# Attention and a gated feed-forward block on one core: query and key transposes of the later tiles moved from TensorE to DMAs, in a newly planned order

## The chip, the cores and the metric

One core of a Trainium2 chip. The time is the device's microseconds for one execution, as the median of several runs; "span" is the profiled execution from its first to its last instruction, about 1.8 us shorter than the time. Each kernel was measured in the same rounds, and on the same chip, as the kernel before, and the ratios quoted are to that one (its medians: 271.45 to 271.49). Two other kernels, of different rounds, are compared through it; the last run was on another chip than the rest of the experiments.

## The reference

```python
# q, k, v: (4, 8, 768, 64); heads 0, 2 and 6 see all earlier keys,
# the other five only the first 4 keys and the last 64
scores = q @ k^T / 8, masked; a = softmax(scores)
x = (a @ v) laid out as (3072, 512)
g = x @ w_gate                      # 512 x 1536
silu = g / (1 + exp(-g))
return (silu * (x @ w_val)) @ w_out # 1536 x 512, float32 out
```

The kernel works in fp16 with float32 sums. Attention is cut into 12 pairs of 128-query tiles (24 tiles); four tiles make a group, and the feed-forward products of a group run on TensorE between the attention work of later tiles.

## The kernel before

Every instruction is a named task. A planner, run beforehand, fixed the order of all tasks (`ORDER`) and for each task the engine that does it (`WAYS`); the kernel holds both as encoded strings and issues accordingly, so each engine's instruction stream is fixed. The parts that matter here:

```python
XBAR = 12                      # tiles from 12 on: output transposed by a DMA on SyncE
RINGS = {"raw": 11, "hq": 2, "e": 7, ...}   # buffers in rotation

def cast(n, kd, j):            # q or k of pair n: float32 as loaded -> fp16 in hq
    ...
    copy(T_c[n, kd, j], hqs[n][:, "qk".index(kd), j]..., r[:, :, j]...)

def transposes(n, w):          # w = 0: queries, 1: keys; 8 transposes on TensorE
    for j in range(2):
        for p in range(4):
            nc.tensor.transpose(tr[...], hqs[n][:, w, j, p // 2, ...], ident)

def evac(n):                   # PSUM -> qT, its two half-zero copies (one each)
    copy(T_ev[n, 0], qT[n % 2][0:64, 0]..., trs[n, 0][0:64])
def evac1(n):
    copy(T_ev[n, 1], qT[n % 2][64:128, 1]..., trs[n, 0][64:128])
def evack(n, x, ps):           # PSUM -> kT
    ...
# small copies that gather sink and window blocks (names used below):
#   sk, sv   sinks of k and v       pk, pv   previous blocks of k and v
#   cx       v as loaded -> fp16    ex       exponentials (ScalarE only)
#   mask     product of e with a mask
```

A task's `ways` say which engines could do it: `copy` tasks may go to ScalarE, VectorE or GpSimd, exponentials only to ScalarE.

The softmax here doesn't subtract the row's maximum and nothing guards it: scores larger than these inputs give would overflow.

Of the kernel before, what the change touches and what calls it, by code (L numbers as in the profile page):

```python
# [16 lines left out]
    "000701060803091Ixq040A1J1L1K02050By81T1V1N1O0C1Uy81Q1o1S1R1M0D2cxy1W1p1r1q1w1X0E1z1P1x1e1y2d2021"  # L17
    "0G1Y1g1Z1f1v1a4D1b1h0H1txs1i101c1s1j220F1d1k2Y2X231l0Pxs1m2a1u242A2514130I1n26272Z9c2B9m280N9w11"
    "9n292E9d9o2C9e4E9x0L2F9f2D9p9y9g9z2b0J9q2G4AA0A62H49A94B0M2IA72JA8xo9h1A0KAA9r9i9k9s9j179tA10O9l"
    "AB4CA29uACA3ADA40Q1D1G9vAE160RAFAG1CA5AL480SAH2KAJAM19AI2LAK0T2S2MAQ2T2N1F2UAR0U2RAN2Q2V2P2WAO3M"  # L20
    "2OAS0V2g2e3L38ATAP2h39AV0X3A2jAU3BAa2i2k0a3G3C3F2mAY3I2n3D0WAW3H2o152u2fAX3J0Y3E2pAd2v1EAZ3K0c2x"
    "Ab122yAcAf2l0b18302w2q31Ai0Z2rAg3N3PAe3v322s3QAkAh2z0dAj3w3O3SAl33An3T2tAp1B0e1H43Am3VAq34453R3W"
    "As0f443y3XAu353U3YAo3x360g3Z42373f403a463g3zAvAr0hAt4G3i3b473jAw3c4w0i4F3h3dAx3l4jAz3k3m0j3e3pB0"
    "4k3q4p414r4l0k3n5WB13o4n4s4HB24x3r4m4tB44I5Y0l4u4K4o3s5dB55c4v4L0m4z3tB63u4J4NBE0n4O4yBJ625X5bBH"
    "630oBF4VBKBG4M5e4WBL4P0pBM685a4Y69BOBI674ZB3BN4qBTBP6L64BRBQBU4Q664bBWBV4cAy4a5g4RBYBS4S504XBZBb"
    "BX51BaBd5ZBc5253B75fBgBeB8Bf4TB9655A54BA0q5B5672BBBhBiBn55BjBC0r57Bl6sBo4d58594eCC6v0s6uBk5G4fBp"
    "6t5HBsBm0t6N744gBx4U5C5IBy0u4h5DBqBt4i5JBu5hBD5KBr5QBvBz5MBwC05N0v5iC25L6o5OC1C35ECD6r6p5PC55R5j"
    "5F0w5SC46qC76K5T5kC65UCAC87e5V7fC96ACW7g0xCB8C8OCbCX6CCZCY0y5lCeCcCECd7d0zCaCg8ACf89ClCh8QCjCi8B"
    "5rCFCq955sCHCG6BCr8wCk8x6D8yCm5mCI6E5n5t716w5uCJCn5v6M8vCo5x5wCtCK7Z5yCLCM7aCp975z6xCsCN606G6FCv"
    "Cu7cD06ICwCy6H6JCx6OD1COCz6PD25oD36Q5p6R7bD45qD56SDAD66T6UD8DBD76VDC6W6b6XDD6cD9DF616d6eDGDIDECP"  # L30
    "6jDHCRDK6k6f6y6YDN6Z6h6a6g6z6iCS7085DJ75DLCT8788766l868GCUDPDM6m78CQDQDSDO79776nDU8H7B947kDR7CDV"
    "DT7F737l7DDW7E7A8P7KDX7h7G7LDZCV7j7H7NDY7I8rDo7O8tDa8N7P7iDr7Q8u7M7JDbDp7RDqDtDsDy8sDuDwDc7U8D7V"
    "DeDvDd7SDf8EE3Dz7TDgE08FE8DxE47mE5E1E97WEAED7n7XE6E2EE7o8zEFEIE7EBEJEGEKEC7p7Y7uEN7vEHEL7qEOEQDh"
    "7xEP7w7rDj91ES7sDiEMDkETER7t7y80EUEX907zEc81EYDlEd828J8IEeEV8KEZDm8R83Eh8M8S84EaEW8UEbEiEm8L8VEj"
    "Ef8T8XEk8Y8e928f8ZEnEg938gF6FBElF78h8WFGFCF8EoFD96F9FHFIFEDnFAFLFF8iFJ8aFM8m8j8k8nFQ8lFN8b988cFV"
    "99FK8oFR9BFOFWFS9CFXFT8d9AEpFaFU9DErFbFP9E8pEs9I9FEtFYEu9GFd9HEq9N9J8qEwFc9K9OEx9L9P9QFf9R9XFZEy"
    "9Y9SFkEvEzFe9TFgF0Fp9UFhF19MFqFl9VFi9WF29ZFmF39aFnFr9bFjFsF4FuFtG4FoFvFzG5G0FxFwF5G2G1FyGOG3GTGP"
    "G6GQGUGYGVG7GRGZG8G9GSGdGaGAGeGWGfGbGXGgGcGBGhGiGCGnGlGjGEGkGoGpGsGmGxGtGqGuGyGvGzGrH2GwH7H3H0H8"
    "H4GFH9GDH5HAH6H1GGHBHCHHHDHFHEGHHMHGGIHIHKHJHNHLHOHPHRGJHSGKHTGLHQHUHWHVHXGMHYGNHbHZHcHaHdHeHf"
)  # L40
WAYS = (
    "000000000000000000000000000000000000000000000000000000000000000001002010021000112002001001000100"
    "000000000000000020011000001000000000000000000000100011100000010011101100100100000000001000000000"
    "000100100000000000000000000000000000010000000000000000000110000001000001100100000000000000000000"
    "000000000000001000001000000000000000000000010000000000101011010000000100000000001000001101000000"
    "100101000000000000000000000100000000000100001001000111100000100000000000000000000000000000011011"
    "000000000000000000000010101010100001000101000000100000000000000000000011020100110110100010000000"
    "000000010000000000000000000000000000000000000000000000000000000000000000000000000000000000000000"
    "000000000000100000000010000000000000000000000000000000000000000000000000000000000000000000000000"
    "000000000000000000000000000000000000000000000000000000000000000000000000000000000100000000000000"  # L50
    "000000000000000000000000000000000000000000000000000000000000000000000010000000000000000000000000"
    "000000000000000000000000000000000000000100000000000000100000000000000000000000000000000000000000"
    "0000000000000000000000000000100001000000"
# [55 lines left out]
def kernel(  # L109
# [37 lines left out]
    HALVES = 4  # L147
    NG = len(SIZES)
# [8 lines left out]
    RINGS = {"raw": 11, "hq": 2, "e": 7, "xb": 3, "xt": 2, "sig": 2, "sil": 3, "ahead": 3,  # L157
             "h": 2 * NJ, "osb": 2, "gv": 3, "o": 1, "sc": 1, "av": 1, "tr": 1}
# [100 lines left out]
    def mask_fill():  # L259
        ps = mask_ps.pop()  # L260
        for dst, src in ((m2[:, 0:1], OWN), (m2[:, 1:4], DIAG), (m2[:, 4:5], FAR),
                         (m1[:, 0:2], OWN), (m1[:, 2:4], FAR),
                         (m0[:, 0:2], DIAG), (m0[:, 2:7], BAND0), (m0[:, 7:8], DIAG)):
            nc.vector.tensor_scalar(  # L264
                out=dst, in0=ps[:, src].unsqueeze(1).to_broadcast([128, dst.shape[1], 128]),
                scalar1=-1.0 / OFF, op0=ALU.mult, scalar2=1.0, op1=ALU.add)
# [6 lines left out]
    qT = [const.tile([128, 2, 4, 2, 128], FH, name=f"qT{n}") for n in range(2)]  # L273
    k2 = [const.tile([128, 4, 4, 128], FH, name=f"k2_{n}") for n in range(2)]
# [12 lines left out]
    def fill2():  # L287
        for n in range(2):
            nc.vector.memset(k2[n], 0.0)  # L289
            nc.vector.memset(v2[n], 0.0)  # L290
# [13 lines left out]
    T_fill2 = P.add("fill2", [("DVE", 4.0, 4.0, 0)], -0.5, fill2, after=[T_fill0])  # L304
    T_mord = P.add("mord", [pe(0.216)], -0.5, mask_order, deps=[T_masks], takes=["tr"])
    T_fill = P.add("mfill", [("DVE", 2.4, 2.4, 0)], -0.4, mask_fill, deps=[T_mord])
    P.uses(T_mord, "tr", T_fill)
# [32 lines left out]

    T_load, T_seq = {}, {}
    T_dma = P.add("dma", [("SP", 4.8, 4.8, 0)], -9.0, lambda: None)
    for at, (kd, n) in enumerate(order):
        d = {"q": 1.78, "k": 1.78, "x": 1.78}.get(kd, 1.42)
        T_load[kd, n] = P.add(
            f"load {kd}{n}", [("SP", d, d + (0.9 if at < 5 else 2.0), 0)], at * 1e-2 - 5,
            (lambda kd=kd, n=n: load(kd, n)), after=[T_dma, T_seq.get("load") if kd in "qkx" else None],
            takes=["raw"], grp=f"L{n if kd in 'qkx' else kd}")
        if kd in "qkx":
            T_seq["load"] = T_load[kd, n]  # L350
# [4 lines left out]
    def wcast(kind, n):  # L355
        r = landed.pop((kind, n))
        if kind == "o":
            dst, src = wo_sb[:, 2 * n:2 * n + 2, :], r.rearrange("p (a n) -> p a n", a=2)
        else:
            dst = (wg_sb if kind == "g" else wv_sb)[:, :, n * 256:(n + 1) * 256]  # L360
            src = r.rearrange("p (a n) -> p a n", a=4)
        copy(T_w[kind, n], dst, src)

    for n in range(6):
        for kd in "gvo":
            pos = 0.9 + n / 10 if kd == "o" else n / 6 - 0.3
            T_w[kd, n] = P.add(
                f"wc {kd}{n}", [pool(1.04), act(1024), both(0.75)], pos,
                (lambda kd=kd, n=n: wcast(kd, n)), deps=[T_load[kd, n]])
            P.uses(T_load[kd, n], "raw", T_w[kd, n])  # L370


    A = 0.25

    XBAR = 12

# [9 lines left out]
    def cast(n, kd, j):  # L386
# [3 lines left out]
        r = landed[kd, n].rearrange("p (h j d) -> p h j d", j=2, d=64)  # L390
        copy(T_c[n, kd, j],
# [4 lines left out]
    def castv(n, m, j):  # L396
# [3 lines left out]
             r[m * 64:(m + 1) * 64, :, j])  # L400

# [16 lines left out]
    def evac(n):  # L418
        copy(T_ev[n, 0], qT[n % 2][0:64, 0].rearrange("c p j n -> c j p n"),
             trs[n, 0][0:64])  # L420
# [6 lines left out]

    def evac1(n):
        copy(T_ev[n, 1], qT[n % 2][64:128, 1].rearrange("c p j n -> c j p n"),
             trs[n, 0][64:128])  # L430
# [26 lines left out]
    def plan(t):  # L457
# [3 lines left out]
        if i == 0:  # L461
            at = enumerate(((0, 0), (2, 2), (3, 4), (1, 6)))
            return [([(p, (0, 1), c, 0) for _, (p, c) in at], 8, m0)]
# [16 lines left out]
    def marks(t, u):  # L480

        if t >= LEAD:
            return []
        if TILES[t][1] == 0:
            return [(0, DIAG, 2), (2, BAND0, 2), (4, BAND0, 3), (7, DIAG, 1)]
# [18 lines left out]
    scs, whole_sc, es, av_blocks = {}, {}, {}, {}  # L504

    def scores(t, u, unit):
        if (t, u) == (1, 0):
            sc = [buf("gv", [128, 4, 128], FP, "sc") for _ in range(2)]
# [3 lines left out]
        scs[t, u] = sc  # L512
# [14 lines left out]
    def exps(t, u, unit):  # L527
        sc = scs.pop((t, u))
# [6 lines left out]
        if (t, u) == (1, 0):  # L535
            for x in range(2):
                nc.scalar.activation(
                    out=e[:, 4 * x:4 * x + 4], in_=sc[x], func=AF.Exp, scale=scale)
        else:
# [384 lines left out]
```

## Time and profile before

271.49 us (271.47 to 271.74, 3 runs), span 269.7 us. The table gives the first four stretches of 20 us. "Wanted" TensorE work is the count of matmuls of each shape in the stretch, times (columns / 2400 + 0.0025) us, without the filler matmuls; matmuls shown on the edge of a stretch count in both, so a stretch can read up to 0.4 us too high. The other columns are busy time.

| stretch, us | TensorE wanted | ScalarE | GpSimd |
|---|---|---|---|
| 0 to 20 | 6.27 | 11.18 | 13.23 |
| 20 to 40 | 14.73 | 16.10 | 14.92 |
| 40 to 60 | 18.30 | 19.68 | 14.85 |
| 60 to 80 | 19.18 | 17.70 | 12.99 |
| every later full one | 20.1 to 20.5 | | |

### The profile page before, as it was taken

To read this page: it belongs to the slowest core of one execution; us is meant where nothing else is said; L and a number is where in the kernel's file an instruction comes from. 1 tells how busy PE (TensorE), PEld (TensorE's weight loads), DVE (VectorE), ACT (ScalarE), POOL (GpSimd) and SP (SyncE) were. 2 spreads that over 40 slices of the span, in tenths; PEclk is the share of its full clock that TensorE was granted. 3 is DMA by queue.
4 is the path that set the end of the run, shared out by engine and by line. 5 is a ranking of instruction groups with operands and counts; after the bars stand their busy time and mean duration, and the time that the engine had idled before them with its cause. 6 is when DMAs were issued, how large, how long until landed. Compare 5 with 4: busy or idle time off the path is not lost.

```text
span 269.7 us, 5353 instructions
## 1 busy us (share of the span) xinstructions
PE 257.9 (96%) x2063; PEld 150.2 (56%) x2063; DVE 173.6 (64%) x340; ACT 167.1 (62%) x260; POOL 113.0 (42%) x145
## 2 busy tenths in 40 slices
PE   7799889899999999999999999999999999999993
PEld 7777546465655565455566655555555554444441
DVE  6757787896679487666668257764582565555321
ACT  2499779999897668767757974486564613141300
POOL 6679936774786541876523233366320200000000
PEclk9999999999999999999999999999999999999999
DMA  7999999999950999011114210102014220110144
GB/s 193 295 347 349 332 280 357 341 288 290 289 158 11 256 310 277 8 40 41 39 21 98 61 39 19 41 19 62 1 23 96 59 59 3 39 39 0 41 102 93
DMA packets 55801, 36.52 MB, mean 135 GB/s; under 512 B 8160, under 2 KB 51168, under 8 KB 55776
## 3 DMA queue, kind: packets, MB, share of 16 engines
q1 hardware_dynamic: 55696, 36.05, 50.4%
q8 instruction: 16, 0.26, 0.4%
q10 hardware_dynamic: 80, 0.13, 0.2%
q14 instruction: 9, 0.07, 0.1%
HBM read 28.31 MB, written 6.29 MB: 128 GB/s over the span
## 4 chain that ended last, share of the span: by engine, by line
PE 80%; ACT 12%; DVE 5%; issue 2%; ACTq 0%
PE gv L761 42%; PE o_ps L790 21%; PE sc L524 9%; PE av L557 5%; ACT e L540 4%; PE tr L413 3%; ACT v L178 2%; ACT hq L178 2%; ACT sig L767 1%; ACT vt L178 1%; DVE m L264 1%; PE xtr L582 1%; DVE v L290 1%; DVE k L289 1%; DVE wg_sb L180 1%
## 5 line engine op out<-in xcount | busy, mean ns | idle before, releaser
L540 ACT ACTIVATE e<-sc 128x1024 f16<-128x1024 f32 (+4 forms) x67 | 60.9, 909 | 22.9 <-PE sc L524 22.5
L761 PE MATMUL gv<-xt,wg_sb 128*128 128x512 f16 (+1 forms) x304 | 71.7, 368 | 1.7 <-DVE wg_sb L180 1.2
L761 PE MATMUL gv<-xt,wv_sb 128*128 128x512 f16 (+1 forms) x304 | 72.3, 368 | 0.0
L548 POOL TENSOR_TENSOR e<-e,m 128x640 f16<-128x640 f16 (+1 forms) x25 | 44.5, 1787 | 66.0 <-ACT e L540 65.9
L790 PE MATMUL o_ps<-wo_sb,h 128*128 128x512 f16 x288 | 71.8, 379 | 0.3 <-ACT o_sb L178 0.3
L767 ACT ACTIVATE sig<-gv 128x512 f32<-128x512 f32 (+1 forms) x76 | 43.1, 575 | 44.6 <-PE gv L761 42.6
L771 DVE SCALAR_TENSOR_TENSOR sil<-sig,gv 128x512 f32<-128x512 f32 (+1 forms) x76 | 49.5, 656 | 31.6 <-ACT sig L767 31.1
L778 DVE SCALAR_TENSOR_TENSOR h<-sil,gv 128x512 f16<-128x512 f32 (+1 forms) x76 | 48.8, 655 | 9.6 <-PE gv L761 8.5
L761 PEld LDWEIGHTS <-wg_sb 128*128 128x128 f16 x304 | 28.9, 98 | 29.3 <-DVE wg_sb L180 1.4
L761 PEld LDWEIGHTS <-wv_sb 128*128 128x128 f16 x304 | 28.7, 98 | 26.6 <-issue 0.2
L790 PEld LDWEIGHTS <-h 128*128 128x128 f16 x288 | 26.6, 98 | 26.3 <-issue 0.5
L524 PE MATMUL sc<-qT,kT 128*128 128x256 f16 (+1 forms) x228 | 35.2, 257 | 1.4 <-ACT e L540 0.8
L180 POOL COPY v<-vt 32x528 f16<-32x528 f16 (+1 forms) x46 | 29.4, 639 | 6.5 <-ACT vt L178 3.8
L524 PEld LDWEIGHTS <-kT 128*128 128x128 f16 x228 | 20.6, 98 | 13.3 <-issue 2.7
L180 POOL CAST vt<-raw 64x512 f16<-64x512 f32 x30 | 18.6, 623 | 16.1 <-DMA raw<-in_v_dram 11.2
L557 PEld LDWEIGHTS <-e 128*128 128x128 f16 x472 | 20.1, 97 | 7.5 <-issue 0.5
L565 DVE RECIPROCAL rc<-av 128x4 f32<-128x4 f32 x48 | 8.6, 180 | 24.0 <-PE av L557 23.6
L178 ACT CAST hq<-raw 128x512 f16<-128x512 f32 x32 | 19.3, 617 | 4.3 <-DMA raw<-in_q_dram 3.0
L557 PE MATMUL av<-vt,e 128*128 128x65 f16 x392 | 21.7, 193 | 0.2 <-DVE xb L566 0.2
L566 DVE TENSOR_TENSOR xb<-av,rc 128x256 f16<-128x256 f32 x48 | 20.4, 424 | 1.7
L413 PE MATMUL tr<-ident,hq 128*128 128x128 f16 x192 | 15.0, 219 | 2.1 <-DVE m L264 1.0
L413 PEld LDWEIGHTS <-hq 128*128 128x128 f16 x192 | 12.2, 98 | 5.7 <-DVE m L264 1.2
(57 smaller groups left out, 191.8 us busy)
## 6 DMA issues: line engine op xcount, KB each, us to landing
raw<-in_q_dram SPq DMA_DIRECT2D x12, 512.0 KB, 7.2
raw<-in_k_dram SPq DMA_DIRECT2D x12, 512.0 KB, 7.1
raw<-in_v_dram SPq DMA_DIRECT2D x12, 512.0 KB, 7.4
out_dram<-o_sb SPq DMA_DIRECT2D x47, 128.0 KB, 2.3
raw<-in_moe_w_gate_dram SPq DMA_DIRECT2D x6, 512.0 KB, 8.7
raw<-in_moe_w_val_dram SPq DMA_DIRECT2D x6, 512.0 KB, 8.7
raw<-in_moe_w_out_dram SPq DMA_DIRECT2D x6, 512.0 KB, 7.5
xt<-xb SPq DMA_TRANSPOSE x12, 2.4
```

Of the source, the lines that this page charges most:

```text
L178: nc.scalar.copy(out=dst, in_=src)
L180: ENG[task.way[0]].tensor_copy(out=dst, in_=src)
L413: nc.tensor.transpose(tr[:, p, :, j, :] if w else tr[:, j, p, :], hqs[n][:, w, j, p // 2, (p % 2) * 128:(p % 2 + 1) * 128], ident)
L524: nc.tensor.matmul(sc[c // 4][:, c % 4:c % 4 + n, :], weights, moving, start=first, stop=last)
L540: nc.scalar.activation(out=e[:, 0:n], in_=whole_sc.pop((t, u))[:, 0:n], func=AF.Exp, scale=scale)
L548: ENG[task().way[0]].tensor_tensor(out=ev, in0=ev, in1=mm, op=ALU.mult)
L557: nc.tensor.matmul(av[:, n, 0:65], ee, vv, start=(m == 0), stop=(m == len(bl) - 1))
L761: nc.tensor.matmul(ps, wsb[:, kk, j * 128:(j + 1) * 128], xt[:, kk, c[0]:c[1]], start=(kk == 0), stop=(kk == 3))
L767: nc.scalar.activation(out=sg[g, j, c], in_=gs[g, j, c], func=AF.Tanh, scale=0.5)
L771: nc.vector.scalar_tensor_tensor(out=sl[g, j, c], in0=sg.pop((g, j, c)), scalar=1.0, op0=ALU.add, in1=gs.pop((g, j, c)), op1=ALU.mult)
L778: nc.vector.scalar_tensor_tensor(out=hs[g, j][:, c[0]:c[1]], in0=sl.pop((g, j, c)), scalar=0.5, op0=ALU.mult, in1=vs.pop((g, j, c)), op1=A ...
L790: nc.tensor.matmul(o_open[g, tt], hs[g, j][:, tt * 128:(tt + 1) * 128], wo_sb[:, j, :], start=(j == 0), stop=(j == NJ - 1))
```

## The change

Intent: take the transposes of the late pairs off the full TensorE and give them to DMAs, which issue from SyncE and write straight to SBUF. Queries of pairs 5 to 11 and keys of pairs 8 to 11 go this way (the outputs of the last twelve tiles already did). The plan was made anew, with SyncE's issue and the transfer behind it costed apart, and with smaller units at the start.

```diff
 ORDER, WAYS: all new
-    RINGS = {"raw": 11, "hq": 2, "e": 7, ...}
+    RINGS = {"raw": 11, "hq": 2, "e": 6, ..., "queue": 4}
+    hqz = const.tile([128, 2, 2, 4, 128], FH, name="hqz")   # zero-padded queries
+    XQK = 5
+    XK = 8
 def cast(n, kd, j):
+        if n >= XQK and kd == "q":
+            for s_ in range(2):        # two half-size casts, each into its padded place
+                copy(T_c[n, kd, j], hqz[:, j, s_]..., r[:, :, j]...)
+            return
+    def dmaq(n, j):
+        nc.sync.dma_start_transpose(
+            out=qT[n % 2][:, :, :, j].rearrange("c s p n -> c (s p) n"),
+            in_=hqz[:, j].rearrange("p s a x -> p (s a x)"))
+    def dmak(n, j):
+        ...
+        for m in range(2):
+            nc.sync.dma_start_transpose(out=kT[b % 2][:, :, at:at + 64],
+                in_=hqs[n][m * 64:(m + 1) * 64, 1, j].rearrange("p r x -> p (r x)"))
 # at the start: tiles 0 and 1 scored in half-size units; first gate and value
 # weights cast in halves; memsets of k2, v2 split into four (one on GpSimd);
 # normalisations of tiles 0 to 3, and copies of transposed outputs, may go to
 # ScalarE; pair 2's loads ahead of most weight loads
```

## The prediction

> **What bounds the kernel now.** I read the page first (busy shares, slices), then the stretches of 20 us, then the chain of waits, then TensorE's waits and the transposes' own row. The page says that TensorE is the engine to look at, and that its clock is granted in full throughout:
>
> ```profile
> PE 257.9 (96%) x2063; PEld 150.2 (56%) x2063; DVE 173.6 (64%) x340; ACT 167.1 (62%) x260; POOL 113.0 (42%) x145
> PE   7799889899999999999999999999999999999993
> ACT  2499779999897668767757974486564613141300
> PEclk9999999999999999999999999999999999999999
> DMA  7999999999950999011114210102014220110144
> ```
>
> The reader should see two stages: up to about slice 12 (80 us) TensorE has holes while ScalarE and the DMAs are near full; from there TensorE is full and nothing else is. The stretches say the same in microseconds:
>
> ```profile
> 20.00:40.00 20.00, 17.33 (x168) 12.13 (x166) 15.20 (x37) 16.10 (x28) 14.92 (x22) 1.00 1.09 321
> 40.00:60.00 20.00, 19.06 (x174) 11.46 (x173) 17.42 (x32) 19.68 (x31) 14.85 (x17) 1.00 1.12 328
> 80.00:100.00 20.00, 20.00 (x179) 11.86 (x178) 14.80 (x32) 14.51 (x23) 12.13 (x10) 1.00 0.68 177
> 200.00:220.00 20.00, 20.00 (x153) 10.90 (x152) 10.76 (x23) 9.20 (x14) 3.09 (x2) 1.00 0.26 59
> ```
>
> "Busy" TensorE need not be TensorE at its rate, so I checked the rate. In the timeline, 8 transposes start at 56.17 and the next matmul at 56.62: 0.45 us for eight, 56 ns each, although the table below gives 219 ns as the length of one. In the chain, 56 projections of 512 columns take 12.10 us, 216 ns each. Both fit columns/2400 us plus 2.5 ns. With that spacing and the counts by shape the whole program is: 832 full-width projections 179.6, 64 of 256 columns 7.0, 196 score products of 256 columns 21.4 and 80 of 128 columns 4.5, mask products 2.3, 472 value products 14.0, 192 transposes of queries and keys 10.7, 48 of outputs 2.7, together **242.3 us** of wanted work (156 filler matmuls apart). TensorE's last matmul ends at 265.1 us in the chain of waits. So 22.8 us of TensorE time are lost. Counting the same way by stretch, 13.7 us are lost before 20 us, 5.3 in 20 to 40, 1.7 in 40 to 60, 0.8 in 60 to 80, and nothing measurable after that: each later stretch of 20 us holds 20.1 to 20.3 us of work. TensorE's waits confirm that they are few and early:
>
> ```profile
> PE gv L761 <- DVE wg_sb L180: 1.2, 1, 1.2
> PE tr L413 <- DVE m L264: 1.0, 1, 1.0
> PE sc L524 <- ACT e L540: 0.8, 2, 0.6
> PE tr L413 <- ACT sig L767: 0.7, 1, 0.7
> ```
>
> **What the Trainium skill says.** "VectorE: DVE Perf Modes", The three transpose paths, gives 390 ns for one 128x128 transpose on TensorE and 1309 ns by DMA, so one by one the DMA looks worse. The trace agrees that a single DMA transpose is slow (2.4 us from issue to landing, but for four blocks), yet in this pipeline a TensorE transpose holds TensorE for 56 ns, not 390; that is what counts here. "TensorE: Matmul & The Clock Gate", Part 4: PE-mode transpose, adds that the result goes to PSUM and needs a copy after; the trace shows those copies (0.69 us on VectorE, 1.00 us on ScalarE for half a pair's queries). "DMA: Bandwidth & Descriptors", Issuing engines are not separate DMA queues, says that all DMAs share the 16 DMA engines and interleave; here loads of 512 KB take 7.1 to 8.7 us to land when they queue, so a transpose issued among loads may land late. No run yet shows that.
>
> **The change part by part.** First, what it removes from TensorE. Pairs 5 to 11 lose the 8 query transposes each (56), pairs 8 to 11 the 8 key transposes each (32): 88 of 192, confirmed by the instruction order of the changed kernel, which has 40 + 64 left. 88 x 56 ns = **4.9 us**. Where they lie:
>
> ```profile
> L413 PE MATMUL tr<-ident,hq 128*128 128x128 f16 x192 | 15.0, 219 | 2.1 <-DVE m L264 1.0 <-ACT sig L767 0.7
> 80.00:120.00 40.00, 2.44 (x32) 2.12 (x32) 1.00 0.59 152
> 120.00:160.00 40.00, 3.05 (x40) 2.43 (x40) 1.00 0.23 49
> 160.00:200.00 40.00, 1.22 (x16) 1.06 (x16) 1.00 0.13 29
> ```
>
> (the last three are the transposes alone, by stretch). 88 transposes run after 80 us now, which is nearly the removed set: in a stage where TensorE never waits, each comes off the end one for one. The outputs' twelve DMA transposes are already in the kernel before; nothing is gained there.
>
> Second, the copies. Fourteen query and four key evacuations go; fourteen casts become 28 half-size ones into a zero-padded buffer. By the instruction counts and the rows' means ScalarE ends with about 3 us more, because copies of v move to it (v copies of 32 and 2 partitions go from 18 to 28, 0.62 us each) and evacuations leave it; VectorE about equal (nine more masks, eight fewer casts, fewer evacuations), GpSimd loses nine masks. After 80 us these engines have 5 us or more free in almost every stretch, so this is worth nothing there.
>
> Third, what it adds: 14 query transposes of 256 KB and 16 key transposes of 64 KB on SyncE's queue.
>
> ```profile
> xt<-xb SPq DMA_TRANSPOSE x12, 2.4
> 166.36 1.19 SPq L576 DMA_TRANSPOSE xt<-xb  x1
> raw<-in_q_dram SPq DMA_DIRECT2D x12, 512.0 KB, 7.2
> ```
>
> An issue holds SyncE 1.19 us; if that doesn't grow with the size, 30 more are 36 us of SyncE, which is idle most of the time from 105 us on. Landing, an estimate: 2.4 us for 128 KB, near 3 us for 256 KB, more behind loads. The pair's queries are double-buffered, a pair lasts some 19 us, so there is room if the order issues them in time; nothing of this should lie on the path.
>
> Fourth, the start. Tiles 0 and 1 are scored in half-size units, the first gate and value weights cast in halves, memsets split and one given to GpSimd, four normalisations moved to ScalarE, pair 2's loads put before most weight loads. Walking the first engines by the rows' durations: VectorE saves one 0.94 us memset before the masks but makes nine mask instructions for eight, so the first query transposes start near 9.8 us instead of 10.69; 46 fillers then stand before the first scores (18 before), 2.6 us, so these start near 13.0, as now (13.13). From there smaller units bring the first value product about 1 us sooner. Then ScalarE decides: summing its instructions up to a given exponential and setting TensorE's wanted work beside it, the new order cannot lose less than about 20 to 21 us on ScalarE's account (66.0 us of ScalarE work plus 8.3 us of early idling against 53.3 us of TensorE work, around tile 7). The kernel before loses 22.8. So 2 us at most are to be had at the start; I take 1.4, a choice, because a planner chose this order and ScalarE will not be without holes.
>
> **Sum.** 271.5 - 4.9 - 1.4 + 0.3 for a few late transposes = **265.5 us**.
>
> **The rivals.** (a) The wait takes the place: a transpose lands late behind loads, or SyncE's in-order queue holds it behind a store that waits. For it: the queue's waits are long already (SyncE waits 36.4 us in total for ScalarE's output copies alone), and some of the query transposes are issued among the last loads. Against: those waits are the order's slack, and the twelve present transposes never stop TensorE. If it holds for half the pairs at 1 us each, the time is 268 to 269. (b) ScalarE becomes the bound for longer: more ScalarE work falls before tile 7 than now. Then the start costs 1 to 2 us more, and the time is 267 to 268. (c) The start gains much more than I allow, because ScalarE now idles about 15 us in the first 60 and a better mix removes that: 262 to 263. (d) The transposes were hidden anyway: spoken against by the full stretches after 80 us; it would leave 270.
>
> **Range and chances.** The TensorE saving is firm to 0.5 us; the start lies between -2 and +3 around the middle, stalls between 0 and 3. Range 262.5 to 268.8. Two per cent is 266.06, only 0.5 us above the middle: faster 0.58, same 0.40, slower 0.02.
>
> **What would show it.** Right: 88 fewer transposes on TensorE, all stretches after 80 us still full, the last projection group of the same length, end near 258.7 on TensorE and 263.7 in the span. Wrong: TensorE waits on a DMA of the query or key transposes (rival a), TensorE's loss before 80 us above 23 us with ScalarE full (rival b) or below 19 (rival c). A query transpose that holds SyncE for twice 1.19 us would upset the issue estimate, though not yet the end.

## More of the kernel before

Except where a run is called slow, all runs quoted were fast.

The chain that ended last, as the page of the kernel before gives it:

```profile
PE 80%; ACT 12%; DVE 5%; issue 2%; ACTq 0%
```

## The result

**268.42 us** (268.26 to 268.90, 4 runs) against 271.48 us in the same rounds: a ratio of 0.9889, 95% interval 0.9872 to 0.9906. (A ratio is the mean time of one kernel's fast runs over that of the other's of the same rounds, so not quite the ratio of the medians.) The gain is 3.1 us, where the prediction had 6.0; it lies within the range, at its upper end.

The page of the kernel after, to be laid beside the lines that the prediction shows (busy times, then the slices of ScalarE and GpSimd):

```profile
PE 254.4 (95%) x1984; PEld 146.4 (55%) x1984; DVE 171.6 (64%) x345; ACT 171.0 (64%) x283; POOL 92.3 (35%) x126
...
ACT  3799999999999874895696555665443643423000
POOL 8748866445358323388003230520122020000000
```

In the eleven slices from the third on ScalarE now reads 9 without a gap; before, it had three 7s and an 8 among them. GpSimd, on the other hand, has lost 20.7 us in the whole. The stretches (length, then busy time of TensorE, its weight loads, VectorE, ScalarE, GpSimd, the granted clock, DMA share, GB/s) give the same:

```profile
20.00:40.00 20.00, 16.71 (x168) 12.69 (x169) 12.82 (x34) 19.58 (x39) 15.72 (x22) 1.00 1.11 322
40.00:60.00 20.00, 19.59 (x152) 11.22 (x151) 15.57 (x29) 19.10 (x28) 10.88 (x11) 1.00 1.05 315
60.00:80.00 20.00, 18.96 (x189) 11.89 (x187) 12.57 (x29) 19.45 (x32) 9.31 (x14) 1.00 1.06 285
```

ScalarE is busy 58.1 of these 60 us, against 53.5 before; GpSimd 35.9, against 42.8. The wanted TensorE work in the four first stretches is 6.38, 13.83, 19.68 and 18.28: 21.8 us lost before 80 us, 21.5 before. The chain of waits points to who sets the pace:

```profile
PE 71%; ACT 17%; DMA 3%; SPq 3%; issue 2%; DVE 1%; ACTq 0%
```

ScalarE's share of the chain rose from 12 to 17%, TensorE's fell by 9 points. Followed in time, from 18.5 to 39 us it is ScalarE's almost alone; some of its pieces (start, length, instruction):

```profile
25.88 0.63 ACT v L183
26.52 0.63 ACT v L183
27.18 0.66 ACT sig L881 x2
27.83 0.92 ACT e L604
```

Small copies of v (2 or 32 partitions, yet 0.63 us each) and an exponential stand one after the other. Over the first 80 us the groups by line show these copies, first of the kernel before, then of the kernel after:

```profile
L178 ACT COPY v<-vt 2x528 f16<-2x528 f16 (+1 forms) x10 | 6.3, 626 | 0.1
```

```profile
L183 ACT COPY v<-vt 2x528 f16<-2x528 f16 (+1 forms) x16 | 10.0, 627 | 0.3
```

These copies are 3.7 of the 7.1 us by which ScalarE's busy time of the first 80 us grew (64.7 to 71.7); casts, normalisations and copies of transposed outputs are most of the rest.

TensorE's own waits stay short, and none in the list names a DMA:

```profile
PE gv L875 <- DVE sil L885: 1.3, 3, 0.6
PE sc L594 <- ACT e L604: 1.2, 4, 0.4
```

The DMA transposes, from issue to landing in us (median):

```profile
kT<-hq SPq DMA_TRANSPOSE x16, 2.4
qT<-hqz SPq DMA_TRANSPOSE x14, 3.4
```

One issue held SyncE for a median of 1.31 us (queries, 256 KB) or 1.24 us (keys, 64 KB). The medians hide a tail: the slowest query transpose landed after 8.0 us, and GpSimd waited 11.7 us in total before casts into the single padded buffer `hqz` for the transpose that still read it. None of this reached TensorE, whose listed waits from 80 to 170 us are 0.2 us in total.

**Where the time went.** Wanted work of the program: 242.3 - 88 x 0.0558 = 237.4 us. TensorE ends at 262.0 us (265.1 before), so it lost 24.6 us, before 22.8: 4.9 saved, 1.8 given back. Of this 1.8, the stretches place 0.3 before 80 us and 0.75 in 100 to 120 and 140 to 160 us (19.81 and 19.73 us of wanted work, before 20.23 and 20.06), where the chain runs through ScalarE's casts, copies and exponentials again. The remaining 0.75 is hidden by the double counting at the edges. Counted once each by their start, the matmuls place 0.3 before 80 us, 1.2 in 100 to 160 us (58.44 us of wanted work, before 59.63), and small pieces elsewhere. The 4.9 itself is an account, 88 times the spacing; no run isolates it.

### The profile page after: what moved, and what is told of

The parts are those of the page before. It is cut to its first block, busy times and chain, and to the rows that moved or that the text cites. A ratio compares the mean times of both kernels' runs of the same rounds, so it can differ in the third digit from the quotient of the medians.

```text
span 266.5 us, 5265 instructions
## 1 busy us (share of the span) xinstructions
PE 254.4 (95%) x1984; PEld 146.4 (55%) x1984; DVE 171.6 (64%) x345; ACT 171.0 (64%) x283; POOL 92.3 (35%) x126
## 4 chain that ended last, share of the span: by engine, by line
PE 71%; ACT 17%; DMA 3%; SPq 3%; issue 2%; DVE 1%; ACTq 0%
PE gv L875 40%; PE o_ps L904 20%; PE sc L594 7%; ACT e L604 5%; ACT v L183 4%; PE av L624 4%; DMA raw<-in_v_dram 3%; ACT vt L183 2%; ACT hq L183 2%; SPq L330 2%; ACT sig L881 2%; SPq L338 1%; ACT k L183 1%; PE tr L472 1%; ACT wo_sb L183 0%
## 5 line engine op out<-in xcount | busy, mean ns | idle before, releaser
L604 ACT ACTIVATE e<-sc 128x1024 f16<-128x1024 f32 (+4 forms) x71 | 62.2, 880 | 26.3 <-PE sc L594 25.9
L875 PE MATMUL gv<-xt,wv_sb 128*128 128x512 f16 (+1 forms) x304 | 70.8, 368 | 1.3 <-DVE sil L885 1.3
L875 PE MATMUL gv<-xt,wg_sb 128*128 128x512 f16 (+1 forms) x304 | 70.6, 368 | 0.6 <-DVE xt L185 0.5
L612 POOL TENSOR_TENSOR e<-e,m 128x640 f16<-128x640 f16 (+1 forms) x16 | 27.5, 1716 | 69.4 <-ACT e L604 54.3
L594 PEld LDWEIGHTS <-kT 128*128 128x128 f16 x228 | 20.5, 98 | 12.8 <-issue 2.3
L624 PEld LDWEIGHTS <-e 128*128 128x128 f16 x472 | 20.1, 97 | 8.2 <-ACT e L604 0.9
L185 POOL COPY v<-vt 32x528 f16<-32x528 f16 (+1 forms) x36 | 22.4, 621 | 4.6 <-ACT vt L183 2.5
L185 POOL CAST vt<-raw 64x512 f16<-64x512 f32 x23 | 15.8, 689 | 20.9 <-DMA raw<-in_v_dram 16.3
L624 PE MATMUL av<-vt,e 128*128 128x65 f16 x392 | 21.8, 193 | 0.5 <-ACT e L604 0.4
L641 DVE TENSOR_TENSOR xb<-av,rc 128x256 f16<-128x256 f32 x47 | 19.8, 424 | 1.6
L183 ACT CAST hq<-raw 128x512 f16<-128x512 f32 x28 | 16.9, 617 | 4.4 <-DMA raw<-in_q_dram 3.6
L185 DVE COPY o_sb<-o_ps 128x512 f32<-128x512 f32 x14 | 9.6, 688 | 14.4 <-PE o_ps L904 14.4
L612 DVE TENSOR_TENSOR e<-e,m 128x1024 f16<-128x1024 f16 (+1 forms) x22 | 14.7, 670 | 6.3 <-ACT e L604 6.2
```

The source lines that it names most:

```text
L183: nc.scalar.copy(out=dst, in_=src)
L185: ENG[task.way[0]].tensor_copy(out=dst, in_=src)
L594: nc.tensor.matmul(sc[c // 4][:, c % 4:c % 4 + n, :], weights, moving, start=first, stop=last)
L604: nc.scalar.activation(out=e[:, 0:n], in_=whole_sc.pop((t, u))[:, 0:n], func=AF.Exp, scale=scale)
L612: ENG[task().way[0]].tensor_tensor(out=ev, in0=ev, in1=mm, op=ALU.mult)
L624: nc.tensor.matmul(av[:, n, 0:65], ee, vv, start=(m == 0), stop=(m == len(bl) - 1))
```

## The experiments

My theory after the result (A): the DMAs do what they should, and the loss is ScalarE's: the new plan gave it work that GpSimd could do, in the stage where its exponentials set the pace. The rivals put the loss on the DMAs and on SyncE's queue, in whole or in part. The expectations name what each makes of a run. All kernels gave correct results. The plans are encoded, so the edits of order and engine are listed by task. Runs go by short labels: e1 and e1b have the DMAs in the old order, e2 and e2b the transposes back on TensorE, e3 and e4 copies off ScalarE, e6 to e8 copies at chosen places.

### The DMAs alone, in the order of before

```diff
 # kernel before, its ORDER and WAYS
+    XQK, XK = 5, 8       # cast, dmaq, dmak as in the change; key transposes issued
+                         # right behind their casts, query ones at the old evacuations
-    "raw": 11, "e": 7
+    "raw": 10, "e": 6    # room for two padded query buffers
 moved: ex10.3 behind val9.0, sc11.0 behind ex10.3 (the smaller ring needs it)
```

> The kernel before with the DMA transposes alone: queries of pairs 5 to 11 and keys of pairs 8 to 11 go by DMA, in the order of the kernel before, start untouched (two padded buffers, e ring 6 and raw ring 10 to make room, one exponential moved by eight places). Theory A (each removed transpose comes off the end, and what the change lost it lost at its replanned start and in ScalarE): 271.5 - 4.9 = 266.6, between 266.0 and 267.2, better than the changed kernel's 268.4. Rival B (the DMA transposes land late and cost TensorE some 2 us): 268 to 269, with TensorE waiting for qT or kT. Rival C (making room in the rings costs something): TensorE waits early, on loads or exponentials, above 267.5.

Measured: 278.37 us (278.02 to 279.70) against 271.45; ratio 1.027, interval 1.0251 to 1.0289. That is slower than the kernel before, and far from theory A's number. SyncE's timeline shows why (start, length, instruction):

```profile
96.47 0.53 SPq L326 DMA_DIRECT2D raw<-in_k_dram  x1
104.25 2.50 SPq L421 DMA_TRANSPOSE kT<-hq  x2
106.80 0.57 SPq L326 DMA_DIRECT2D raw<-in_v_dram  x1
```

SyncE works its queue in order. A key transpose waited for its cast until 104.25, and the load behind it was issued at 106.80; in the kernel before it was issued at 96.53. The casts of this v came late, and with them TensorE, which stopped twice for over 3 us (wait: total, times, longest):

```profile
PE sc L564 <- ACT e L580: 5.0, 5, 3.3
PE gv L801 <- DVE sil L811: 4.3, 3, 3.5
```

The first stop (110.9 to 114.4 us) is this load's: ScalarE waits 3.4 us to cast its v, and the activation that TensorE's next products need stands behind that cast. The second (until 155.3) is a late transpose itself: ScalarE waits for transposed keys before the next exponential.

```profile
ACT k L178 <- DMA kT<-hq: 4.0, 1, 4.0
```

The stretches 100 to 120 and 140 to 160 hold only 14.93 and 14.98 us of wanted work. A hole also costs more than its length: after each, the granted clock fell to half for some 3 us (below, an average over 2 us).

```profile
114.00:116.00 2.00, 1.57 (x4) 0.56 (x4) 2.00 (x4) 0.77 (x2) 1.08 (x2) 0.52 1.16 282
116.00:118.00 2.00, 2.00 (x7) 0.80 (x6) 0.86 (x2) 0.00 (x0) 1.39 (x3) 0.63 1.08 232
```

Columns are those of the stretches above; the clock is the third number from the right. "TensorE: Matmul & The Clock Gate", Part 1: The HAM clock gate, says that TensorE's clock goes to half after an idle window of about 3.4 us; this trace agrees (TensorE stood idle for 3.54 and 3.31 us before the two drops to 0.50). So without a new order the DMAs do harm, through SyncE's queue. This is the prediction's rival (a), in both its forms, which did not reach TensorE in the planned kernel.

### The same with another place in SyncE's queue

```diff
 # previous kernel
-key transposes right behind their casts
+issued behind later tasks of SyncE: q5 behind load k8; q7 and k8 behind load x11;
+k9 behind the output transpose of tile 14; q9 and k10 of tile 15; k11 of tile 16
 moved: both casts of q7 behind load k8; pk3.1 to pk3.3 behind the transpose of tile 17
```

> As e1_before_plus_dma (278.4 us), but the transposes stand elsewhere in SyncE's queue: those of pairs 5, 7, 8 behind the loads that they had held up, those of pairs 9 to 11 behind an output transpose that is ready earlier; three copies of keys on ScalarE are moved behind them. Theory A2 (e1 lost 12 us because a transpose that waits for its cast holds the loads behind it in SyncE's in-order queue; the DMA work as such is free): most of that comes back, 266.5 to 269, TensorE's waits behind loads gone. Rival (the DMA work itself, or the padded casts, cost TensorE time wherever they stand): stays above 274.

Measured: 272.85 us (272.20 to 272.98 in five fast runs; a sixth, slow, took 278.55) against 271.49; ratio 1.0048, interval 1.0036 to 1.006. Moving the transposes in the queue took back 5.5 us, so the queue was most of the loss. Yet it lies between the two expectations (266.5 to 269, and above 274) and above the kernel before, with new waits:

```profile
PE o_ps L840 <- ACT o_sb L178: 3.6, 3, 1.7
```

Holes remain in 60 to 80 (17.47 us of wanted work) and 140 to 180 us (17.57 and 18.57). The queue still has a part in the later ones: in the chain from 142.5 to 158 us SyncE issues one transpose after the other, the output stores stand behind them, and ScalarE waits 4.4 us for such stores before it can empty PSUM for TensorE. I did not find a placement by hand that shows the 4.9 us in the old order. So "the DMAs alone are worth 4.9" was not seen in this order. The next pair of runs takes them out of the new order instead.

### The transposes back on TensorE, in the order of after

```diff
 # kernel after
 def dmaq(n, j):          # second call of a pair only
-        nc.sync.dma_start_transpose(...)
+        8 x nc.tensor.transpose(tr[...], hqz[...], ident)
+        2 x nc.vector.tensor_copy(qT..., tr...)
 def dmak(n, j):          # likewise
+        8 x nc.tensor.transpose(...); 1 x nc.vector.tensor_copy(kT..., tr...)
 # cast: both half-size casts of a query go to one unpadded place in hqz
```

> The changed kernel with its 88 DMA transposes put back on TensorE, at the places where the DMAs stood, with the copies on VectorE; everything else of the replanned order stays. Theory A: 268.4 + 4.9 = 273.3, up to 274.5 where TensorE now waits for a cast. Rival B (the DMAs cost about what they save in stalls): 270 to 271.5.

Measured: 280.78 us (280.50 to 280.97); ratio 1.0346, interval 1.0333 to 1.0359. Six us more than expected. But here TensorE, also in order, transposes at the early places at which DMAs were to be issued, so it may wait for casts. (The trace, read afterwards, names no cast among TensorE's waits; the longest after 80 us are behind VectorE.) The next kernel moves them as late as their users allow.

```diff
 # previous kernel
 moved: dq5 to dq11 to shortly before the first scores of their pair (and before the
 next pair's query casts), dk8 to dk11 to shortly before the first pk that reads them
```

> As e2_after_on_tensor (280.8 us), but the TensorE transposes stand as late as their users allow instead of at the DMAs' places, so that TensorE doesn't wait for casts. Theory A: 268.4 + 4.9 plus some waits, 273 to 276: the DMAs are worth about 5 us in this order. Rival (the replanned order can't do without the DMAs, since TensorE and VectorE have no room for transposes and copies there): stays near 280.

Measured: 279.02 us (278.77 to 279.18); ratio 1.0278, interval 1.0265 to 1.0292: near the rival's 280, not theory A's 273 to 276. Against this form the DMAs are worth 279.0 - 268.4 = 10.6 us. 4.9 of it is TensorE's work. The rest shows mostly as waits behind VectorE, which now makes the copies out of PSUM (busy 184.1 us, 171.6 in the kernel after):

```profile
PE gv L890 <- DVE h L907: 2.5, 3, 1.3
PE gv L890 <- DVE sil L900: 2.2, 3, 1.4
```

That VectorE makes nearly all of these copies is this test's own choice, and part of the price: in the kernel before, ScalarE made 8 of the 18 such copies after 80 us. A form that shares them out was not run. Between 80 and 160 us its four stretches hold 73.9 us of wanted work, the kernel after 80.0: 6.1 us of holes. So an order planned for one form can't be used to price the other: kernel before and kernel after are each fitted to their own, and the mixed ones lose both ways. That the DMAs hold the kernel after back, nothing in these runs supports.

### ScalarE relieved early

```diff
 # kernel after
-ScalarE: cx2.0.0, cx2.0.1, cx2.1.1, cx3.1.0, cx3.1.1, cx4.0.0, cx4.1.1, cx6.0.1,
-         cx6.1.0, pv0.2, pv0.4, pk0.3, pv1.2, pv1.3, sv1.3
+GpSimd:  the same
 moved: sv1.1 to sv1.4 (all on GpSimd now) behind the fourth output weight cast
```

> The changed kernel with copies moved from ScalarE to GpSimd in the first 80 us only: six casts of v, copies of v and k for tiles 4 to 11, and the four sink copies of batch 1 moved later on GpSimd; about 12 us of ScalarE work. Theory A (ScalarE is the bound from 18 to 78 us): the loss before 80 us falls from 21.8 to 18 to 20, time 265 to 266.8. Rival (the loads or VectorE set the pace there, ScalarE is only full beside them): no faster than 268. Rival (GpSimd becomes late with masks): slower than 268.4.

Measured: **266.44 us** (266.39 to 267.91); ratio 0.9835, interval 0.9817 to 0.9854. Expected 265 to 266.8: theory A holds. Nothing but the engine and the place of small copies and casts changed (nine casts of v, where the expectation says six), and 2.0 us of the kernel after came back. The stretch 20 to 40 us:

```profile
20.00:40.00 20.00, 17.46 (x175) 13.31 (x175) 14.29 (x36) 17.26 (x32) 14.88 (x22) 1.00 1.12 325
```

ScalarE is busy 17.26 us in it, in the kernel after 19.58. In the first 80 us it does 62.1 us instead of 71.7, and TensorE's loss there falls from 21.8 to 19.9 us: the 2 us.

### More of the same

```diff
 # previous kernel
-ScalarE: cx9.0.1, cx10.0.0, cx10.0.1, cx11.1.0, sv2.2, sv3.1, sv3.2, pv2.4, pv3.2, pv3.4
+GpSimd:  the same, at their places
```

> As e3_after_act_early, and ten more tasks of ScalarE after 80 us (copies of v, casts of v) on GpSimd. Theory A: the holes that TensorE has between 100 and 160 us behind ScalarE close as well, 0.5 to 1 us below e3. Rival (those holes come from late DMA transposes or from the score ring): equal to e3 within 0.2 us.

Measured: 268.06 us (267.79 to 269.91); ratio 0.9889, interval 0.9868 to 0.991. Expected was a further gain; it lost 1.6, so neither theory A nor the rival was tested: GpSimd, also in order, now comes late with its masks:

```profile
PE av L624 <- POOL e L612: 3.8, 3, 1.8
```

The stretch 120 to 140 holds only 18.46 us of wanted work. So a copy must not only go to the idler engine, but to a place where it does not delay something that TensorE wants.

### Relief at chosen places

```diff
 # e3's kernel
+ScalarE, behind the second output weight cast: sv0.1, sv0.2
+GpSimd, behind the fourth output weight cast: sv0.3, sv0.4, sv1.1, sv1.2
+GpSimd, before pv2.1 and pv2.2: sv1.3, sv1.4
+VectorE instead of GpSimd: the mask of tile 6
+GpSimd, behind masks 10.1, 11.0, 15.0 and sv2.1: pv2.1 to pv2.4, sv2.2, cx10.0.*, pv3.1 to pv3.4
+GpSimd: cx11.1.0
```

> As e3_after_act_early (266.4 us), with GpSimd kept in time: sink and window copies of v moved to where GpSimd idles and shortly before their users, one late mask given to VectorE, and the copies that crowd ScalarE at 108 to 111 and 131 to 138 us put on GpSimd after its masks. Theory A (ScalarE crowded, then GpSimd late, are what is left of the loss): 264 to 265.8, TensorE's wait of 1.3 us for a mask gone, the stretches 100 to 160 at 20.2 or more of wanted work. Rival (the start is held by loads): 266.0 or more.

Measured: **265.73 us** (264.95 to 267.72, six runs); ratio 0.9798, interval 0.977 to 0.9826. From 40 us on TensorE is nearly full (20.23, 19.75, 20.40, 20.03 ...), so the late holes behind ScalarE are nearly gone: 100 to 160 us holds 20.03, 20.20 and 19.94 (expected 20.2 or more), or 59.31 us counted by start, where e3 has 58.22. The wait of 1.3 us for a mask is gone too. In time the gain over e3 (0.7 us) is not clear of the noise, as the intervals of the two ratios overlap. The stretch 20 to 40, though, fell to 13.07 us of wanted work (13.83 in the kernel after, 15.24 in e3's). The trace shows a half-rate clock there:

```profile
35.00:36.00 1.00, 1.00 (x10) 0.87 (x9) 0.34 (x2) 0.21 (x1) 0.94 (x3) 0.50 0.90 258
```

The clock is 0.50 from 34.0 to about 37.4 us, after 3.4 us in which TensorE's records cover about half (30.6 to 34.0). That costs up to 1.7 us, an estimate: half of these 3.4 us. Not every run has it: runs with a mean clock of 0.99 took 266.30 and 266.37, three with 0.996 to 1.0 took 264.95 to 265.15 (and one with 0.998 took 267.72, unexplained).

A variant tests whether the late first load of pair 1's v, seen in the chain of the kernel after (9 us from issue to landing), is to blame:

```diff
 # e6's kernel
 moved: load x1 one place earlier, ahead of a gate weight; that weight's cast behind cx1.0.0
```

> As e6_after_relief, with the load of pair 1's values one place earlier (before the second gate weight block), as the changed kernel had put two weight loads before it and it landed at 18.4 us. Theory (that landing is on the path, ScalarE then waits 0.6 us): 0.3 to 1 us below e6. Rival (ScalarE's backlog hides it): equal to e6 within 0.2 us, or a little slower from the later gate block.

Measured: 265.75 us (265.16 to 266.45, 4 runs); ratio 0.9793, interval 0.9776 to 0.981. The load did land 1.75 us sooner (16.71 us, 18.46 in e6), and the time is the same. At a like clock (0.996 to 1.0) two runs took 265.16 and 265.46, e6's three 264.95 to 265.15: no gain of 0.3 us shows. That load is hidden, as the rival said, though the chain named it.

### Relief with the start of e3

```diff
 # e6's kernel
-the moves of sv0.1 to sv0.4
+sv0.1 to sv0.4 as in the kernel after
```

> The version of e6_after_relief with one thing put back: the four sink copies of v for batch 0 stay on the places and engines that the changed kernel gives them (e6 had moved them to ScalarE behind the first output weight cast and to GpSimd). Relief theory: e3 held 15.24 us of wanted TensorE work in 20-40 us, e6 only 13.07, and e6 held 1.5 us more than e3 in 40-80 us and 0.6 more after. If the moved sink copies (and the clock of 0.91 that e6's trace shows in 20-40 us) are what cost e6 the 2 us at 20-40, this kernel has both gains: 264.0 to 265.0, with 15 us in 20-40 and over 39.5 in 40-80. Rival: TensorE work pulled forward in 20-40 is only taken out of what can be done before tile 7 on ScalarE's account; then 40-80 gives it back and the time stays at 265.5 to 266.5 like e3 and e6.

Measured: **264.69 us** (264.23 to 265.74); ratio 0.9758, interval 0.9734 to 0.9781. The time is as the first theory said, and the work of both gains is there:

```profile
20.00:40.00 20.00, 17.45 (x175) 13.30 (x175) 14.26 (x36) 17.26 (x33) 14.76 (x22) 1.00 1.10 319
```

Wanted work is 15.24 us in 20 to 40 and 39.3 in 40 to 80 us (e3's 38.45; expected was over 39.5); the clock is full. TensorE loses 19.1 us before 80 us. How much of the step from e6 (1.0 us by the medians) is the sink copies' and how much the clock's is not separated: e6's profile had the half-rate stretch and this one has not. At a like clock the two differ by some 0.5 us (264.23 to 264.84 against 264.95 to 265.15); this kernel's one run at 0.992 took 265.74. It is the fastest kernel of the study, 3.7 us below the change and 6.8 below the kernel before, with nothing added to the change but other engines and places for small copies and one mask.

## Why the prediction was right or wrong

The time fell in the range, but 2.9 us above the expected 265.5, and the likelier class (over 2% faster) did not come. The large term held and two smaller ones both missed upward, so that it stayed inside is owed to the range's width. Step by step:

- **What bounds the kernel: right.** TensorE from 80 us on, ScalarE before; that the loads bind too, as it thought, no run shows. Two readings were slightly off: later stretches hold 20.1 to 20.5 us, not 20.3, and in the first 60 us ScalarE idled 13.0 us, not "about 15".
- **88 transposes, 4.9 us: right in this order.** The instruction count and the sum hold, as an account: 3.1 us gained plus 1.8 us of further holes. The two runs with the transposes put back cost 10.6 us and more, as VectorE's copies came on top; that the copies were worth nothing because both kernels' own orders had room for them is argued, not shown.
- **Late transposes, +0.3; rival (a): right for this order.** No TensorE wait on a DMA; issue 1.31 and 1.24 us instead of the 1.19 assumed; landing 3.4 us instead of "near 3", and 8.0 at worst. That rival (a) is real was shown in the old order: 278.37 us, of which 5.5 went with the queue's order (and the few tasks moved with it).
- **The start, -1.4: this step failed.** Its first half came true: first query transposes near 9.8 us (measured 9.64), first scores near 13.0 (12.88), first value product about 1 us sooner (14.57, before 15.93). What failed is how near ScalarE lets the kernel come to the bound of 20 to 21 us of loss. That ScalarE decides was right, and so was its early idling (8.3 us foreseen; 7.9 up to the last exponential of tile 7). But by that exponential TensorE had lost 21.9 us, in the kernel before 22.2. Before 80 us it lost 21.8, 0.3 more than before instead of 1.4 less, so the term was 1.7 us off. The 22.8 that the bound was set against is also the whole program's loss, of which the prediction's own stretches put only 21.5 before 80 us: there was less room than "2 us at most".
- **ScalarE after 80 us, "worth nothing there": failed too, by about 1.2 us.** The prediction looked at the sum of free time in a stretch; in 100 to 120 and 140 to 160 us the chain runs through ScalarE's in-order runs of copies and casts ahead of an exponential, though ScalarE is only 14.77 and 11.72 us busy in them. The relieved kernels bear it out: counted by start, 100 to 160 us holds 58.44 us of wanted work in the kernel after, 58.22 in e3, 59.31 and 59.30 in e6 and e8, which move copies there too; before it was 59.63. The two terms, 1.7 and 1.2, are the whole error of 2.9.
- **The comparison that misled.** The prediction summed ScalarE's work up to tile 7 for the new order, but did not lay the same sum of the old order beside it. Up to that exponential ScalarE is busy 63.2 us, in the kernel before 54.9; in the first 80 us it had 7.1 us more (71.7 against 64.7), while GpSimd had 6.6 us less. This is the mechanism of rival (b), given as 267 to 268, and the time lies just above it, but its sign, a loss above 23 us before 80 us, did not come. The first relieved kernel shows the cause: with about 10 us of small copies and casts off ScalarE, the loss before 80 us is 19.9 us, 1.6 less than in the kernel before: about the 1.4 that the prediction had booked.

## What to carry to other kernels

When a change rearranges work, sum each engine's work up to the moment at which the bounding stage ends, in the old order and in the new one, and compare the two: 3.9 us more on ScalarE over the whole program was 7.1 us more in the one stage that could not take it. A DMA transpose relieves a full TensorE and the engine that empties PSUM, but here it stood in its issuing engine's in-order queue: issue it where its input is ready, or it holds back the loads and stores behind it (one load by 10.3 us). Small copies belong on the idlest engine, at a place behind what the full engine is waiting for: ten copies moved without choosing places cost 1.6 us, while seven of them, with places chosen, are part of the fastest kernel.

## What the Trainium skill lacked or had wrong

- "VectorE: DVE Perf Modes", The three transpose paths: compares 390 ns for a 128x128 transpose on TensorE with 1309 ns by DMA, each alone. It leaves out what decided here: among other work a transpose took 56 ns of TensorE's time (a spacing that the skill has elsewhere, for matmuls of this width), and a DMA transpose of 64 or 128 KB took 2.4 us, of 256 KB 3.4 us, from issue to landing.
- "DMA: Bandwidth & Descriptors", Issuing engines are not separate DMA queues: calls the sequencer's time to initiate a DMA "usually small relative to the DMA itself". For DMA transposes it was not: 1.24 us (64 KB) to 1.31 us (256 KB) of SyncE, about half of the former's 2.4 us to landing. That an issue which waits holds back the later loads is not said there; it was a load issued 10.3 us later and a kernel of 278.37 us, 272.85 with another queue order.
- "TensorE: Matmul & The Clock Gate", Part 1: its table names an idle window before the clock halves, and its text short idle spells between groups of matmuls, but no share of busy time at which this happens. Here it halved after 3.4 us in which TensorE's records cover about half the time (0.50 from 34.0 to 37.4 us), in some runs of a kernel and not in others: 266.3 against 265.0 us.
